# A table step at changes of ScalarE's function, and another order of the steps, in an attention and feed-forward kernel

## The chip, the cores and the metric

The kernel runs on one core of one Trainium2 chip. Its time is the device time of one execution in microseconds (us): the median of three runs, of which the lowest and the highest are given as well. A separate execution was taken by the hardware profiler; the rows below come from it. The engines are TensorE (PE for its matmuls, PEld for its weight loads), VectorE (DVE), ScalarE (ACT), GpSimd (POOL) and SyncE (SP, which issues nearly all transfers).

## What is computed

Two attentions after one another for 8 batches of 8 heads (576 rows of 64), then a feed-forward layer with a sigmoid gate over the 4608 rows of 512:

```python
p_packed = sm_attn(p, k, v)          # 32 packed queries look at 576 keys
out = sm_attn(q, p_packed, p_packed) # 576 queries look at the 32 packed rows
x = out.transpose(0, 2, 1, 3).reshape(B * S, H * D)
h = x @ w_in                         # 512 -> 2048
g = h * (1.0 / (1.0 + np.exp(-1.702 * h)))
return (g @ w_out)                   # 2048 -> 512
```

The softmax of `sm_attn` needs the function exp, the gate needs a gelu function. Both are done by ScalarE.

## The kernel before

All the work is one long list of steps, the tuple `order` (from line 931), written out by hand; a loop at the end calls them one by one. Each step puts a few instructions on one engine, and every engine works through its own instructions in that order. Nothing reorders them afterwards, so a step that waits holds up everything behind it on its engine.

A batch `b` goes through these steps. `load` brings k, q and v by DMA on SP's queue. `scores1_mm` (PE) makes the scores of the packed queries, `scores1_copy` moves them to SBUF, `scores1_max` and `bias1` (DVE) find the maxima, `exp1` (ACT) does the exponentials with the row sum. From batch 2 on `turn1_blocks` (DVE), `turn1_out` and `turn1_in` (eight small DMAs out to DRAM and two back) transpose them; then `pack` (PE) multiplies by v, `pack_end` scales, `pack_turn_mm` and `pack_turn_copy` transpose the result `PT`. `scores2_mm` (PE), `scores2_turn`, `max2`, `sub2` (DVE), `exp2` (ACT), `sum2`, `norm2`, `turn2` (DVE) are the second attention, up to its weights in `a` (`a_upper` by ACT, `a_lower` by DVE). `m_mm` (PE) multiplies `PT` by a quarter of w_in, which ACT and DVE then split in two parts (`m_upper`, `m_lower`).

The feed-forward layer runs in two phases of 1024 hidden columns each (first index of a step), per batch, half of the tokens (288) and one of four units `u` of 256 columns. `h_mm` (six matmuls for each half of a unit) fills one of two pairs of PSUM banks, which scores, `pack` and `m_mm` use as well. `g_main` and `g_over` (ACT) apply gelu to 256 and to the last 32 tokens; `g_sum`, `g_upper` (ACT) and `g_lower` (DVE) make and split the blocks of a Strassen-like product, and `prod` (PE) multiplies them by w_out into four accumulator banks A to D; `prod0` does the same plainly for batch 0. Tokens that `g_over` set aside are multiplied under the name "over". `c_take` keeps the sums of the first phase, `c_sum` and `c_comb` (DVE) add them in the second, `store` writes the output.

Weights come in as raw words: `load_w` (SP) into one of two buffers, `begin_w` (ACT) and `join_w` (DVE) turn them into fp32, which frees the buffer for the next `load_w`. `w_diff`, `wa_upper`, `wa_lower`, `wb_upper` and `wb_lower` split and combine w_out.

The function `table` (lines 121 to 123) applies a function to one column of a constant; it is called once, ahead of the list, with exp. Every other load of ScalarE's function table is put in by the compiler ahead of the first instruction that needs the other function.

Of the kernel before, what the change touches and what calls it, by code (L numbers as in the profile page):

```python
# [21 lines left out]
def kernel(  # L22
# [53 lines left out]
    cst = ctx.enter_context(tc.tile_pool(name="cst", bufs=1))  # L76
# [838 lines left out]
    def store(b, half, r=None, block=None, engine=nc.sync):  # L915
# [14 lines left out]
    table(AF.Exp)  # L930
# [34 lines left out]
        (exp2, 0, 1), (h_mm, 0, 0, 0, 0, 1, 1), (join_w, "in", 0, 0, 1), (wa_lower_mm, 0, 0),  # L965
        (load_w, "in", 1, 1, None), (g_main, 0, 0, 0, 0, 0), (sum2, 0, 1),
# [16 lines left out]
        (load_w, "out", 4, 0, None), (g_main, 0, 0, 1, 1), (g0_lower, 0, 0, 1),
        (prod0, 0, 1, 0, 1, 0), (begin_w, "in", 1, 3, None), (g_over, 0, 0, 1, 1),
        (prod0, 0, 1, 0, 0, 1), (g0_upper, 0, 1, 1), (join_w, "in", 1, 3, None),
        (load_w, "out", 5, 0, None), (prod0, 0, 1, 0, 1, 1), (g0_lower, 0, 1, 1), (m_mm, 0, 1),
        (t_store, 0, 1), (scores1_mm, 1, 0), (m_upper, 0, 1), (prod0, 0, 0, 1, 1),
# [795 lines left out]
```

## Time and profile before

| | |
|---|---|
| time, median of 3 runs | 668.72 us (668.45 to 670.74) |
| time of the profiled execution | 671.38 us |
| span of its instructions | 669.6 us |
| PE busy | 657.2 us (98%) |
| DVE busy | 552.0 us (82%) |
| ACT busy | 404.1 us (60%) |
| loads of the function table | 34, of 1.283 us each |

The span begins with the program's first instruction and ends with its last; 1.8 us of the profiled execution lie around it. The busy time of PE comes from modelled ends of pipelined matmuls. The granted clock of TensorE is 1.00 in all the stretches shown that end at 660 us or before, the upper of its two levels (2.4 GHz).

### The profile page before, as it was taken

The numbers are of one execution on the slowest core, as the hardware profiler recorded it, in microseconds if no ns is written. First come the engines' busy times: TensorE is split into PE (matmuls) and PEld (weight loads), VectorE is DVE, ScalarE is ACT, GpSimd is POOL, SyncE is SP. The second block draws the span as 40 slices with busy tenths as digits, with TensorE's granted clock in tenths as the row PEclk, the third lists the DMA queues.
The fourth block names the chain that finished last, engine by engine and source line by source line (L and its number), as shares of the span: only waits on it lengthen the run. The fifth ranks groups of instructions, "written<-read, shape, count | busy, mean of one in ns | idle before, by whom it ended". The sixth has DMA issues, their size and how long they took to land.

```text
span 669.6 us, 15216 instructions
## 1 busy us (share of the span) xinstructions
PE 657.2 (98%) x6227; PEld 597.8 (89%) x6227; DVE 552.0 (82%) x1132; ACT 404.1 (60%) x736; POOL 5.4 (1%) x15
## 2 busy tenths in 40 slices
PE   8999999999999999999999999999999999999997
PEld 6777798989989799798999789999999999999997
DVE  3958998788899887887887866888889978879897
ACT  5867877768576685875866664455444434444441
POOL 2100000000000000000000000000000000000000
PEclk9999999999999999999999999999999999999999
DMA  9876345563565828653576504232243242032422
GB/s 326 323 266 245 134 127 212 149 229 111 153 259 118 305 58 239 216 146 106 176 272 225 183 23 137 101 106 73 105 157 103 56 161 80 32 115 84 143 101 112
DMA packets 59173, 104.91 MB, mean 157 GB/s; under 512 B 31392, under 2 KB 36128, under 8 KB 58208
## 3 DMA queue, kind: packets, MB, share of 16 engines
q1 hardware_dynamic: 58960, 103.81, 47.3%
q8 instruction: 49, 0.80, 0.5%
q14 instruction: 20, 0.16, 0.1%
q10 hardware_dynamic: 144, 0.13, 0.1%
HBM read 70.51 MB, written 33.42 MB: 155 GB/s over the span
## 4 chain that ended last, share of the span: by engine, by line
PE 79%; DVE 8%; ACT 6%; DMA 5%; issue 2%; SPq 0%; ACTq 0%; DVEq 0%
PE h L699 25%; PE accC L860 11%; PE accB L860 11%; PE accA L860 11%; PE accD L860 6%; PE psm_None L547 4%; DMA raw_in_None<-w_in 2%; PE accB_over L860 1%; PE accC_over L860 1%; PE accA_over L860 1%; PE pspv_None L496 1%; PE ps L591 1%; DMA aT<-aside 1%; ACT L719 1%; PE accA L816 1%
## 5 line engine op out<-in xcount | busy, mean ns | idle before, releaser
L699 PE MATMUL h<-a,m 128*128 128x288 f32 x1536 | 226.3, 296 | 1.3 <-ACT over L725 0.6
L699 PEld LDWEIGHTS h<-a,m 128*128 128x128 f32 x1536 | 208.9, 188 | 7.2 <-ACT over L725 1.5
L111 ACT CAST gs<-X 128x896 fp32r<-128x896 f32 (+2 forms) x117 | 105.1, 903 | 70.9 <-DVE X L769 30.2
L789 DVE TENSOR_TENSOR gs<-X,gs 128x896 fp32r<-128x896 f32 x112 | 120.8, 1087 | 25.9 <-ACT gs L111 25.4
L769 DVE TENSOR_TENSOR X<-X 128x256 f32<-128x256 f32 (+1 forms) x336 | 105.2, 330 | 27.0 <-ACT X L719 23.1
L719 ACT ACTIVATE X<-h 128x512 f32<-128x512 f32 (+1 forms) x129 | 75.9, 595 | 71.6 <-PE h L699 45.7
L860 PE MATMUL accB<-Wb,gs 128*128 128x256 f32 x672 | 95.7, 281 | 0.0
L860 PE MATMUL accC<-Wa,gs 128*128 128x256 f32 x672 | 95.4, 281 | 0.0
L860 PEld LDWEIGHTS accC<-Wa,gs 128*128 128x128 f32 x672 | 86.0, 188 | 6.0 <-issue 4.7
L860 PEld LDWEIGHTS accB<-Wb,gs 128*128 128x128 f32 x672 | 86.6, 188 | 2.7 <-issue 1.8
L860 PE MATMUL accA<-Wa,gs 128*128 128x256 f32 x336 | 58.6, 282 | 0.2 <-DVE gs L789 0.2
L860 PE MATMUL accA<-Wb,gs 128*128 128x256 f32 x336 | 57.7, 280 | 0.0
L860 PE MATMUL accD<-Wa,gs 128*128 128x256 f32 x336 | 56.4, 282 | 0.1
L860 PEld LDWEIGHTS accD<-Wa,gs 128*128 128x128 f32 x336 | 46.8, 188 | 5.1 <-issue 4.3
L725 ACT ACTIVATE over<-h 128x64 f32<-128x64 f32 x128 | 34.9, 287 | 26.2 <-PE h L699 25.7
L860 PEld LDWEIGHTS accA<-Wa,gs 128*128 128x128 f32 x336 | 47.9, 188 | 2.8 <-issue 1.3
L860 PEld LDWEIGHTS accA<-Wb,gs 128*128 128x128 f32 x336 | 47.4, 188 | 0.0
L111 ACT CAST m<-psm_None 128x1024 fp32r<-128x1024 f32 x31 | 30.8, 1018 | 14.5 <-PE psm_None L547 14.3
L571 DVE TENSOR_TENSOR m<-psm_None,m 128x1024 fp32r<-128x1024 f32 x31 | 37.4, 1213 | 2.6 <-ACT m L111 2.4
L547 PE MATMUL psm_None<-w_in,PT 64*32 64x512 f32 x496 | 32.4, 596 | 1.3 <-DVE w_in L242 0.9
L665 DVE TENSOR_TENSOR a<-xt,a 128x576 fp32r<-128x576 f32 x31 | 23.1, 749 | 1.8 <-ACT a L111 1.7
L111 ACT CAST a<-xt 128x576 fp32r<-128x576 f32 (+1 forms) x30 | 19.8, 661 | 6.5 <-DVE xt L645 4.0
(203 smaller groups left out, 790.2 us busy)
## 6 DMA issues: line engine op xcount, KB each, us to landing
part<-r SPq DMA_DIRECT2D x14, 896.0 KB, 7.3
p<-part SPq DMA_DIRECT2D x14, 896.0 KB, 5.3
q<-q SPq DMA_DIRECT2D x16, 576.0 KB, 4.6
o<-r SPq DMA_DIRECT2D x16, 512.0 KB, 6.4
raw_out_None<-w_out SPq DMA_DIRECT2D x16, 511.8 KB, 4.7
v<-v SPq DMA_DIRECT2D x7, 1024.0 KB, 9.0
raw_in_None<-w_in SPq DMA_DIRECT2D x12, 511.8 KB, 4.7
k<-pk SPq DMA_DIRECT2D x8, 640.0 KB, 4.4
```

What stands on the lines that cost most here:

```text
L111: nc.scalar.copy(dst, src)
L496: nc.tensor.matmul(bank[32 * j : 32 * j + 32, e, e * D : (e + 1) * D], turned()[:, c, e, 32 * j : 32 * j + 32], vt[:, c, e0 : e0 + D], sta ...
L547: nc.tensor.matmul(banks[eo][32 * j : 32 * j + 32], PT[rows(eo), j, :], w_in_sb[c % 2][rows(eo), j, at], start=True, stop=True,)
L571: nc.vector.tensor_tensor(m[:, 1, :, at], st["bank", "m", b, c, part], m[:, 0, :, at].bitcast(F32), op=ALU.subtract,)
L591: nc.tensor.matmul(bank[32 * j : 32 * j + 32, eo, :NH], st["PT", b][rows(eo), j, :], kq["q0", half][rows(eo), j, :] if b == 0 else kq["q", ...
L665: engine.tensor_tensor(even_odd(a[:, 1], eo), even_odd(st["t", 2, b, half], eo), even_odd(a[:, 0], eo).bitcast(F32), op=ALU.subtract,)
L699: nc.tensor.matmul(h, m[:, part, eo, at], a[:, ap, eo * NH : (eo + 1) * NH], start=(n == 0), stop=(n == len(terms) - 1), skip_group_check= ...
L719: nc.scalar.activation(X[:, :4].rearrange("p (f t) n -> p f (t n)", f=2)[:, chunks(f)], st["h", *k][:, chunks(f), :NM], AF.Gelu_apprx_sigm ...
L725: nc.scalar.activation(over_part(ph, b, half, u), st["h", ph, b, half, u][:, :, NM:NH], AF.Gelu_apprx_sigmoid, scale=2.0,)
L769: engine.tensor_tensor(to, a, b_, op=ALU.subtract)
L789: engine.tensor_tensor(lo, X, hi.bitcast(F32), op=ALU.subtract)
L860: nc.tensor.matmul(acc[:, n * HC : (n + 1) * HC], gs[:, gp, g], Wa[:, wp, w] if w < 4 else Wb[:, wp, w - 4], start=(u == 0 and n == 0 and ...
```

## The change

`table` becomes a step of the list. It applies exp or gelu to one column of the constant `ident` and writes a column of its own, so that it waits for no other engine; nobody reads what it writes. 33 such steps are put into the list, 17 with "gelu" and 16 with "exp". The steps behind some 150 at the start stand in another order; the steps are otherwise the same, with the same arguments, so the matmuls, casts and transfers are the same in number and size. Followed along ScalarE's own steps, the new list has 34 changes of function, as many as the old one. Of these 34 loads one belongs to the call ahead of the list, 18 now fall on a table step and 15 still on the function itself; 15 of the 33 table steps ask for the function that is there already.

The core of the diff: the new function; the opening; batch 1's two attentions; batch 5's transposition; the end.

```diff
-    def table(func):
-        t = cst.tile([P, 1], F32, name="table")
-        nc.scalar.activation(t, ident[:, :1], func)
+    tables = {"exp": AF.Exp, "gelu": AF.Gelu_apprx_sigmoid}
+    primed = cst.tile([P, 2], F32, name="table")
+
+    def table(f):
+        n = list(tables).index(f)
+        nc.scalar.activation(primed[:, n : n + 1], ident[:, :1], tables[f])
...
-    table(AF.Exp)
+    table("exp")
...
-        (prod0, 0, 0, 0, 0, 1), (join_w, "in", 0, 3, 1), (a_upper, 0, 0, 1),
-        (join_w, "in", 1, 0, None), (load_w, "in", 1, 2, None), (prod0, 0, 0, 0, 1, 1),
-        (a_lower, 0, 0, 1), (begin_w, "in", 1, 1, None), (m_mm, 0, 0, 1),
-        (join_w, "in", 1, 1, None), (h_mm, 0, 0, 1, 0, 0), (load_w, "in", 1, 3, None),
-        (m_upper, 0, 0, 1), (wa_upper, 1, 0, 4, dve), (m_lower_mm, 0, 0, 1), (h_mm, 0, 0, 1, 0, 1),
-        (wa_lower, 1), (m_lower_copy, 0, 0, 1), (load, "v", 1, 3), (h_mm, 0, 0, 0, 1, 0),
...
-        (load_w, "out", 5, 0, None), (prod0, 0, 1, 0, 1, 1), (g0_lower, 0, 1, 1), (m_mm, 0, 1),
-        (t_store, 0, 1), (scores1_mm, 1, 0), (m_upper, 0, 1), (prod0, 0, 0, 1, 1),
...
+        (exp2, 0, 1), (table, "gelu"), (h_mm, 0, 0, 0, 0, 1, 1), (join_w, "in", 0, 0, 1),
...
+        (join_w, "in", 0, 3, 1), (prod0, 0, 0, 0, 1, 1), (a_upper, 0, 0, 1), (m_mm, 0, 0, 1),
+        (prod0, 0, 0, 0, 0, 1), (m_upper, 0, 0, 1), (m_lower_mm, 0, 0, 1), (m_lower_copy, 0, 0, 1),
+        (begin_w, "in", 1, 1, None), (join_w, "in", 1, 0, None), (a_lower, 0, 0, 1),
+        (h_mm, 0, 0, 1, 0, 0), (h_mm, 0, 0, 1, 0, 1), (wa_upper, 1, 0, 4, dve), (wa_lower, 1),
+        (join_w, "in", 1, 1, None), (g_over, 0, 0, 1, 0), (g_main, 0, 0, 1, 0),
...
+        (w_diff, 0, 2), (w_diff, 1, 1), (w_diff, 1, 3), (g0_lower, 0, 1, 0), (w_diff, 1, 2),
+        (load_w, "in", 1, 2, None), (load_w, "in", 1, 3, None), (load, "v", 1, 3),
...
+        (join_w, "in", 1, 3, None), (scores1_mm, 1, 0), (m_mm, 0, 1), (g0_upper, 0, 1, 1),
+        (scores1_copy, 1, 0, 0, dve), (scores1_copy, 1, 0, 1), (g0_lower, 0, 1, 1),
+        (wb_upper, 1, 0, dve), (scores1_mm, 1, 1), (m_upper, 0, 1), (scores1_copy, 1, 1, 1),
+        (scores1_copy, 1, 1, 0), (table, "exp"), (scores1_max, 1, 1), (bias1, 1, 1),
...
+        (prod0, 0, 0, 3, 1), (max2, 1, 1), (sub2, 1, 0), (table, "exp"), (wb_upper, 2, 0),
+        (prod0, 0, 1, 2, 0), (wb_lower, 2, 0), (wb_upper, 1, 1), (exp2, 1, 0), (g0_upper, 0, 1, 3),
+        (m_upper, 1, 1), (wb_upper, 0, 1), (m_upper, 1, 0), (wb_upper, 0, 0), (sum2, 1, 0),
+        (g0_lower, 0, 1, 3), (norm2, 1, 0), (prod0, 0, 1, 3, 0), (sub2, 1, 1), (turn2, 1, 0),
+        (m_lower, 1, 0), (c0_take, 0, 1), (a_upper, 0, 1, 0), (a_lower, 0, 1, 0), (c0_take, 0, 0),
+        (h_mm, 0, 1, 0, 0, 0), (h_mm, 0, 1, 0, 0, 1), (m_lower, 1, 1), (exp2, 1, 1),
+        (table, "gelu"), (g_main, 0, 1, 0, 0), (sum2, 1, 1), (g_sum, 0, 1, 0, 0, 1),
+        (g_sum, 0, 1, 0, 0, 2), (g_sum, 0, 1, 0, 0, 3), (h_mm, 0, 1, 0, 1, 0),
...
-        (g_upper, 0, "over", 0, 2, 0, 3), (g_sum, 0, 4, 0, 0, 2), (turn1_blocks, 5, 1),
...
-        (g_main, 0, 4, 0, 2), (turn1_blocks, 5, 0), (norm2, 4, 1), (turn2, 4, 1),
...
-        (pack, 5), (g_over, 0, 4, 1, 1), (g_sum, 0, 4, 0, 3, 3), (g_upper, 0, 4, 0, 3),
...
+        (c_take, 3, 1, "B"), (scores1_mm, 5, 0), (scores1_mm, 5, 1), (scores1_copy, 5, 0, 1, dve),
+        (scores1_copy, 5, 1, 1), (table, "exp"), (g_lower, 0, "over", 0, 2, 3, 7),
+        (scores1_max, 5, 1), (g_sum, 0, "over", 0, 3, 1), (bias1, 5, 1), (exp1, 5, 1),
+        (g_sum, 0, 4, 0, 0, 1), (g_sum, 0, "over", 0, 3, 2), (prod, 0, "over", 0, 1, "C"),
+        (prod, 0, "over", 0, 0, "B"), (prod, 0, "over", 0, 0, "A"), (turn1_blocks, 5, 1),
+        (prod, 0, "over", 0, 1, "D"), (prod, 0, "over", 0, 2, "C"), (prod, 0, "over", 0, 1, "B"),
+        (scores1_copy, 5, 1, 0), (scores1_copy, 5, 0, 0), (g_sum, 0, "over", 0, 3, 3),
+        (scores1_max, 5, 0), (g_sum, 0, 4, 0, 0, 2), (bias1, 5, 0),
+        (g_upper, 0, "over", 0, 3, 3, 7), (g_sum, 0, 4, 0, 1, 1), (norm2, 4, 1),
+        (g_sum, 0, 4, 0, 1, 2), (exp1, 5, 0), (g_upper, 0, "over", 0, 3, 0, 3, dve),
+        (turn1_blocks, 5, 0), (h_mm, 0, 4, 0, 3, 0), (h_mm, 0, 4, 0, 2, 0),
+        (prod, 0, "over", 0, 1, "A"), (table, "gelu"), (turn2, 4, 1),
...
+        (g_sum, 0, 4, 1, 0, 3), (turn1_in, 5, 0), (turn1_in, 5, 1), (pack, 5), (pack_end, 5),
+        (prod, 0, 4, 0, 1, "A"), (pack_turn_mm, 5), (pack_turn_copy, 5, dve),
...
-        (prod, 1, "over", 1, 3, "D"), (c_sum, "over", 1, "B"), (c_comb, "over", 1, 1),
-        (c_sum, "over", 1, "D"), (c_comb, "over", 1, 2), (prod, 1, "over", 1, 0, "C", 0),
-        (prod, 1, "over", 1, 0, "C", 1), (prod, 1, "over", 1, 1, "C", 0),
-        (prod, 1, "over", 1, 2, "C", 0), (c_comb, "over", 1, 3), (prod, 1, "over", 1, 3, "C", 0),
-        (c_comb, "over", 1, 4), (c_sum, "over", 1, "C", 0), (store, 7, 1), (store, "over", 1, 0),
-        (prod, 1, "over", 1, 1, "C", 1), (prod, 1, "over", 1, 2, "C", 1), (store, "over", 1, 1, 0),
-        (c_comb, "over", 1, 5), (prod, 1, "over", 1, 3, "C", 1), (c_sum, "over", 1, "C", 1),
-        (store, "over", 1, 1, 1, act),
...
+        (c_sum, 7, 1, "C"), (c_sum, "over", 1, "A"), (c_sum, "over", 1, "B"),
+        (prod, 1, "over", 1, 0, "D"), (prod, 1, "over", 1, 0, "C", 0), (store, 7, 1),
+        (prod, 1, "over", 1, 1, "C", 0), (prod, 1, "over", 1, 2, "C", 0),
+        (prod, 1, "over", 1, 3, "C", 0), (prod, 1, "over", 1, 1, "D"), (prod, 1, "over", 1, 2, "D"),
+        (prod, 1, "over", 1, 3, "D"), (c_comb, "over", 1, 0), (c_comb, "over", 1, 4),
+        (c_comb, "over", 1, 1), (c_sum, "over", 1, "C", 0), (store, "over", 1, 1, 0),
+        (c_comb, "over", 1, 2), (c_sum, "over", 1, "D"), (c_comb, "over", 1, 3),
+        (store, "over", 1, 0), (c_comb, "over", 1, 5), (prod, 1, "over", 1, 0, "C", 1),
+        (prod, 1, "over", 1, 1, "C", 1), (prod, 1, "over", 1, 2, "C", 1),
+        (prod, 1, "over", 1, 3, "C", 1), (c_sum, "over", 1, "C", 1), (store, "over", 1, 1, 1, act),
```

## Rows read from the trace of the kernel before

**Rows 1.** The page, busy time and share of the span by engine.

```profile
PE 657.2 (98%) x6227; PEld 597.8 (89%) x6227; DVE 552.0 (82%) x1132; ACT 404.1 (60%) x736; POOL 5.4 (1%) x15
```

**Rows 2.** Busy time by stretch (length, PE, PEld, DVE, ACT, POOL, clock, DMA share, GB/s).

```profile
40.00:120.00 80.00, 77.47 (x822) 62.86 (x811) 70.86 (x144) 62.07 (x114) 0.00 (x0) 1.00 0.55 183
...
200.00:300.00 100.00, 97.48 (x1032) 89.23 (x1031) 83.13 (x173) 71.91 (x126) 0.00 (x0) 1.00 0.61 181
300.00:660.00 360.00, 360.00 (x3071) 339.98 (x3070) 299.86 (x601) 185.51 (x329) 0.00 (x0) 1.00 0.36 120
660.00:669.60 9.60, 5.38 (x44) 4.97 (x42) 5.15 (x12) 0.00 (x0) 0.00 (x0) 0.91 0.30 110
```

**Rows 3.** PE in order of time: start, duration, work [idle before <-releaser].

```profile
41.38 0.62 PE L547 MATMUL psm_None<-w_in,PT 64*32 64x512 f32 x2 [0.91 <-DVE w_in L242]
...
53.05 1.87 PE L699 MATMUL h<-a,m 128*128 128x288 f32 x12 [0.40 <-ACT over L725]
...
73.22 1.89 PE L699 MATMUL h<-a,m 128*128 128x288 f32 x12 [0.48 <-DVE m L571]
...
85.94 0.38 PE L860 MATMUL accA<-Wa,gs 128*128 128x256 f32 x1 [0.23 <-DVE gs L789]
...
117.48 0.72 PE L292 MATMUL ps<-k 64*32 64x288 f32 x16 [0.35 <-ACT X L719]
...
219.19 1.32 PE L496 MATMUL pspv_None<-v,aT 128*32 128x64 f32 x80 [1.01 <-DMA aT<-aside]
```

**Rows 4.** PE in order of time, its last five microseconds of work.

```profile
660.72 1.58 PE L860 MATMUL accD_over<-Wa,gs_over 128*128 128x256 f32 x12
662.14 1.92 PE L860 MATMUL accC_over<-Wa,gs_over 128*128 128x256 f32 x15
664.59 1.32 PE L860 MATMUL accC_over<-Wa,gs_over 128*128 128x256 f32 x9 [0.53 <-DVE r_over L899]
```

**Rows 5.** Groups by line, table loads (count | busy us, mean ns | idle before, releasers).

```profile
L719 ACT ACT_TABLE_LOAD x10 | 12.8, 1283 | 5.2 <-PE h L699 5.1
...
L628 ACT ACT_TABLE_LOAD x9 | 11.5, 1283 | 2.9 <-DVE x L624 2.8
...
L389 ACT ACT_TABLE_LOAD x7 | 9.0, 1283 | 5.8 <-DVE nb L373 5.8
...
L725 ACT ACT_TABLE_LOAD x7 | 9.0, 1283 | 1.7 <-DVE gs_over L789 1.5
```

**Rows 6.** ACT in order of time, around two table loads.

```profile
81.77 1.28 ACT L389 ACT_TABLE_LOAD   x1 [0.82 <-DVE nb L373]
83.06 0.78 ACT L389 ACTIVATE x<-x,nb 128x576 f32<-128x576 f32 x1
...
114.30 1.28 ACT L719 ACT_TABLE_LOAD   x1 [2.71 <-PE h L699]
```

**Rows 7.** The chain of waits (start, duration, what) around a table load.

```profile
66.13 0.08 ACT L628
66.21 1.21 issue
```

**Rows 8.** DVE in order of time, ahead of the matmul at 73.22 us.

```profile
68.14 0.75 DVE L633 TENSOR_REDUCE sm<-x 128x18 f32<-128x576 f32 x1 [1.10 <-ACT x L628]
```

**Rows 9.** The chain of waits through w_in's buffers.

```profile
31.57 0.70 DVE w_in L242
...
32.29 7.46 DMA raw_in_None<-w_in
```

**Rows 10.** DVE in order of time, the two steps that split w_out for unit 1.

```profile
32.18 0.69 DVE L113 CAST Wa<-E 128x1024 fp32r<-128x1024 f32 x1
32.90 1.23 DVE L252 TENSOR_TENSOR Wa<-E,Wa 128x1024 fp32r<-128x1024 f32 x1
```

**Rows 11.** The page, DMA issues: size, median time to landing.

```profile
v<-v SPq DMA_DIRECT2D x7, 1024.0 KB, 9.0
```

**Rows 12.** Groups by line, the nearest one to a table step.

```profile
L358 ACT ACTIVATE again<-mx,nb 128x1 f32<-128x1 f32 x2 | 0.6, 284 | 0.0
```

More of the change, by code (lines that the diff above doesn't have):

```diff
@@ new lines @@
+        (begin_w, "out", 4, 0, None), (w_diff, 0, 4), (join_w, "out", 4, 0, None),
+        (h_mm, 0, 0, 0, 2, 0), (h_mm, 0, 0, 0, 2, 1), (exp1, 1, 0), (begin_w, "out", 5, 0, None),
+        (join_w, "out", 5, 0, None), (wb_lower, 1, 0), (h_mm, 0, 0, 1, 2, 0), (g_main, 0, 0, 0, 2),
+        (h_mm, 0, 0, 1, 2, 1), (prod0, 0, 1, 1, 0), (wa_upper, 2, 0, 4, dve), (load, "v", 1, 2),
+        (load, "q", 1, 0), (g0_upper, 0, 0, 2, None, dve), (wa_lower, 2), (g0_lower, 0, 0, 2),
+        (g_over, 0, 0, 0, 2), (g_over, 0, 0, 1, 2), (turn1_last_mm, 1), (g_main, 0, 0, 1, 2),
@@ new lines @@
+        (begin_w, "out", 7, 0, None), (join_w, "out", 7, 0, None), (h_mm, 0, 0, 1, 3, 0),
+        (pack_end, 1), (pack_turn_mm, 1), (wa_upper, 3), (g0_lower, 0, 0, 3), (pack_turn_copy, 1),
+        (w_diff, 2, 4), (h_mm, 0, 0, 1, 3, 1), (g_over, 0, 0, 1, 3), (g_main, 0, 0, 1, 3),
+        (table, "gelu"), (scores2_mm, 1, 0), (load, "q", 1, 1), (wa_lower, 3), (scores2_mm, 1, 1),
+        (prod0, 0, 0, 3, 0), (prod0, 0, 0, 2, 1), (scores2_turn, 1, 0, 1), (scores2_turn, 1, 0, 0),
+        (scores2_turn, 1, 1, 1), (scores2_turn, 1, 1, 0), (m_mm, 1, 1), (m_mm, 1, 0), (max2, 1, 0),
@@ new lines @@
+        (a_lower, 0, 2, 0), (load, "v", 3, 3), (m_lower, 2, 1), (exp2, 2, 1), (load, "k", 3, 0),
+        (h_mm, 0, 2, 0, 1, 0), (h_mm, 0, 2, 0, 1, 1), (load, "k", 3, 1), (t_store, 1, 0),
+        (table, "gelu"), (g_main, 0, 2, 0, 1), (g_over, 0, 2, 0, 1), (begin_w, "in", 2, 0, None),
+        (h_mm, 0, 2, 0, 0, 0), (h_mm, 0, 2, 0, 0, 1), (g_over, 0, 2, 0, 0), (table, "gelu"),
+        (g_main, 0, 2, 0, 0), (prod, 0, 1, 1, 2, "B"), (scores1_mm, 3, 1), (sum2, 2, 1),
+        (norm2, 2, 1), (g_sum, 0, 2, 0, 1, 1), (load, "v", 3, 2), (c_store, 1, 0),
@@ new lines @@
+        (exp2, 3, 1), (table, "exp"), (g_upper, 0, 2, 1, 3), (load, "k", 4, 0), (m_lower, 3, 0),
+        (t_store, 1, 1), (c_store, 1, 1), (load, "k", 4, 1), (a_lower, 0, 3, 0), (m_lower, 3, 1),
+        (h_mm, 0, 3, 0, 0, 0), (h_mm, 0, 3, 0, 0, 1), (table, "gelu"), (h_mm, 0, 3, 0, 1, 0),
+        (h_mm, 0, 3, 0, 1, 1), (g_main, 0, 3, 0, 0), (g_over, 0, 3, 0, 0), (g_lower, 0, 2, 1, 3),
+        (prod, 0, 2, 1, 3, "C"), (table, "gelu"), (g_main, 0, 3, 0, 1), (g_over, 0, 3, 0, 1),
+        (sum2, 3, 1), (g_sum, 0, 3, 0, 0, 1), (scores1_mm, 4, 1), (g_sum, 0, 3, 0, 0, 2),
@@ new lines @@
+        (wa_upper, 6), (m_upper, 0, 3), (m_lower, 0, 3), (m_upper, 1, 2), (m_lower, 1, 2),
+        (w_diff, 6, 1), (w_diff, 6, 3), (w_diff, 5, 4), (wa_lower, 6), (prod0, 1, 0, 1, 0),
+        (prod0, 1, 1, 1, 1), (h_mm, 1, 0, 0, 3, 0), (h_mm, 1, 0, 0, 3, 1), (h_mm, 1, 0, 0, 2, 0),
+        (g_over, 1, 0, 0, 3), (h_mm, 1, 0, 0, 2, 1), (g_main, 1, 0, 0, 3), (g0_upper, 1, 0, 3),
+        (g0_lower, 1, 0, 3), (wb_lower, 5, 0), (wb_upper, 4, 1), (g_main, 1, 0, 0, 2),
+        (g_over, 1, 0, 0, 2), (h_mm, 1, 0, 1, 2, 0), (h_mm, 1, 0, 1, 2, 1), (m_mm, 1, 3),
```

1446 lines of the change are left out of this document (697 added, 749 removed).

## The prediction

> **What bounds the kernel now.** I read first the busy shares: PE is busy 657.2 of 669.6 us, DVE 82%, ACT 60% [rows 1]. The reader sees that only PE's idle time can be won, since no matmul is removed. Second, the stretches: PE is idle 80 - 77.47 = 2.53 us between 40 and 120 us, 2.52 between 200 and 300, nothing between 300 and 660, and 4.22 behind 660 [rows 2]. The opening 40 us are left out, as their steps hardly move. Third, PE's own list, to see what ended each wait [rows 3]: it waits for weights at 41.38 (0.91 us), for ScalarE's gelu at 53.05 (0.40), for DVE's split of m at 73.22 (0.48), for a split block at 85.94 (0.23), for gelu at 117.48 (0.35), and for the transposed exponentials from DRAM at 219.19 (1.01). At the end it waits 0.53 us for `c_sum` [rows 4], and 3.69 us (4.22 less 0.53) of closing work follow its last matmul. So 2.53 + 2.52 + 0.53 = 5.58 us is all that shows as a wait behind 40 us.
>
> A wait costs somewhat more than the idle time shows, since matmul ends are modelled. In the last rows twelve matmuls take 662.14 - 660.72 = 1.42 us, 0.118 each; fifteen more would end their starts at 663.91, but the next start is at 664.59, 0.68 later where 0.53 is shown [rows 4].
>
> **The change, part by part. The loads of the table.** There are 34 before, all of 1.283 us [rows 5], and 34 after, by following exp and gelu along ScalarE's steps in both lists. So nothing is removed. What a table step can do is start a load while ScalarE waits for the data of the function. Before, some loads start only behind that wait: at 81.77 ScalarE has sat idle 0.82 us for `bias1`, loads, and begins exp at 83.06, 0.01 us after the load's end; at 114.30 it had idled 2.71 us for `h_mm` [rows 6]. All idle time ahead of the loads is 5.2 + 2.9 + 5.8 + 1.7 = 15.6 us, and a load can hide at most 1.283 of its own wait. That is ScalarE's time, which is no bound. What reaches PE must be read wait by wait:
>
> - 53.05: `g_over` comes late behind batch 1's two exp1 and two loads. After, exp is loaded behind the score copies; seven such loads before idled 5.8 us [rows 5], about 0.8 each, more than PE's 0.40. I take 0.40, though the gelu load that follows stays at its function.
> - 73.22: the chain runs through the load at 66.13 (0.08 + 1.21) [rows 7] and DVE's 1.10 us wait for exp2 [rows 8] to `m_lower`. After, the load stands ahead of exp2, with `wb_lower` in DVE's gap. I take 0.48.
> - 85.94: the load at 81.77 moves into its 0.82 us of wait [rows 6]. I take 0.23.
> - 117.48: the load at 114.30 had room for all its 1.283 [rows 6]. I take 0.35.
>
> Together -1.5 us. Ends: 0 (something else is late by as much) and -2.1 (0.15 more each). Late next at each is the same work without its load: PE's own queue, or DVE, whose busy share there is 70.86 of 80 [rows 2].
>
> The Trainium skill's page ScalarE: Activation LUTs (Table sets: the hidden batching unit) says that what counts is the number of switches, so calls should be batched by set. By that rule this part is worth 0, the sum without it stands below as a rival. The rows disagree in part: a load is 1.283 whenever it comes, but two of the ones shown come behind idle time.
>
> **Table steps that load nothing.** 15 of the 33 ask for the table that is there. The nearest row is an ACTIVATE on one column with a bias column, 0.284 us [rows 12]; 15 x 0.284 = 4.3 us of ScalarE. The cover is ScalarE's idle time, 17.9 of 80 us between 40 and 120 and 28.1 of 100 between 200 and 300 [rows 2]; without it each would delay by its 0.284 what PE waits for. I take 0; the ends are 0 and +4.3, a gain is excluded since they remove no load. The same page (What ACT_TABLE_LOAD costs) gives 186 ns for an ACTIVATE with immediate scale and bias; by that estimate it would be 15 x 0.187 = 2.8. No run here shows that form.
>
> **Batch 5's transposition.** `pack` waited 1.01 us for `turn1_in` [rows 3]. The new list moves exp's load ahead of the maximum, puts `turn1_blocks` well ahead (between the last of them and `pack`, PE has 14.9 us of matmuls by its pitches, against 7.8 before), and gives PE nine more products between the second `scores1_mm` and `pack`, 9 x 0.118 = 1.06 us. SP's queue has the same eight small DMAs and the q load ahead of `turn1_in`. I take -1.0; ends 0 and -1.2.
>
> **The end.** Before, DVE's `c_sum` of bank C's first half stands behind a queue of combinations when PE wants that bank. After, three D groups, 9 x 0.118 = 1.06 us, stand between the first half's last product and the second half, more than the 0.68 of wait. The closing work is the same. I take -0.6; ends 0 and -0.7.
>
> **The weights at 41.38.** This gets worse. The chain is `join_w` of w_in's tile 1 (31.57 to 32.27), which frees a buffer, then the DMA of tile 3, 7.46 us [rows 9], then its own begin, join and `m_mm`. After, that first `join_w` stands behind `wa_upper` (0.69) and `wa_lower` (1.23) of unit 1 on DVE [rows 10], and its `begin_w` behind the split of m on ACT. Queued behind it are SP's tile 3 and the v load; `m_mm` waits for that. The load leaves some 1.5 us later (1.92 less the half microsecond that DVE had idle). On PE `scores1_mm` now stands ahead of `m_mm` and covers 0.6. I take +0.9. Ends: 0, if the load lands sooner because k is then out of the way, and +3.1, if it takes the 9.0 us of a v load [rows 11] instead of 7.46 (1.5 + 1.5).
>
> **The rest of the order.** What is left, 5.58 - 0.40 - 0.48 - 0.23 - 0.35 - 1.01 - 0.53 - 0.91 = 1.67 us, are other waits. Counted over both lists with PE's pitches, a pair of banks is wanted again within 1.4 us of PE's work in 24 places before and in 21 after, so the new order is about as tight as the old one. I take 0; ends -1.7, all of them gone, and +2, as many new ones.
>
> **Sum.** -1.5 - 1.0 - 0.6 + 0.9 = -2.2 us. The profiled execution, 671.38 us (span 669.6 and 1.8 around it), would become 669.2. The median is 2.66 us below that execution, so the forecast is 668.72 - 2.2 = 666.5 us. On its own it reaches from 664.8 to 668.4.
>
> **The rivals.** *All waits go.* Every wait behind 40 us is filled by the new order: 668.72 - 5.58 = 663.1 us (down to 661.6 if all of them cost 0.68/0.53 of what shows). For it: PE without a wait from 300 to 660 us shows that an order can do this. Against it: the weight chain, and 15 loads that still stand at their function.
>
> *The tables give nothing.* The count of loads is what matters, or another thing is late at each place: 668.72 - 1.0 - 0.6 + 0.9 = 668.0 us. For it: DVE is nearly full between 40 and 120 us. Also in this case: the change doesn't do what it says, as 15 steps load nothing.
>
> *The early load gets in the way.* A table step loads at its place in ScalarE's queue, ahead of casts that PE or DVE need: the one of batch 1 stands in front of `wb_upper` and both `m_upper`. If four of the 18 hold up PE by their whole 1.283, it is +5.1 and the tables give nothing: 668.0 + 5.1 = 673.1 us, slower. It decides from the point where ScalarE has no idle time between the step and PE's next wait for it. For it: most loads before show no idle time ahead of them. Against it: ScalarE is idle 22% and 28% of the time in those stretches [rows 2].
>
> **How the numbers follow.** Forecast 0.46, all waits go 0.25, tables nothing 0.18, load in the way 0.11. The range of 8 in 10 leaves out the upper part of the slow case and the lowest of the fast one: 662.3 to 670.8. This kernel's measurement can tell about 0.5% from no change, 3.3 us: below 665.4 is faster, above 672.1 slower. Faster takes 0.24 of the fast case and 0.08 of the forecast's lower end, 0.32; slower nearly all of the slow case, 0.10; the rest, 0.58, is same.
>
> **What would show it.** Right: 34 loads still, those at a table step starting directly behind the instruction before; PE's idle time between 40 and 120 us near 2.0 and between 200 and 300 near 1.5; no wait at `pack` of batch 5 nor in the last matmuls; a wait near 1.8 at `m_mm` of w_in's second quarter. Wrong: new PE waits of over half a microsecond behind 300 us; casts on ScalarE that wait behind a table load while PE waits for them; a load of tile 3 that lands behind 43 us.

## The result and the profile after

The changed kernel takes 662.17 us (661.84 to 662.21, 4 runs) beside 669.08 (668.45 to 670.74, 4 runs) of the kernel before: a ratio of 0.9892 with a 95% interval of 0.9873 to 0.9911, so 1.1% faster. The forecast was 666.5 us with a range from 662.3 up: the sign was right, the size was not, and the range was missed at its lower end. The most likely case was "same"; "faster" came. The profiled execution took 661.84 us, 660.1 of them the span.

First the busy shares of after, the line that answers to [rows 1], and the busy time by stretch that answers to [rows 2] (length, PE, PEld, DVE, ACT, POOL, clock, DMA share, GB/s):

```profile
PE 652.5 (99%) x6227; PEld 596.8 (90%) x6227; DVE 552.5 (84%) x1132; ACT 408.2 (62%) x769; POOL 5.4 (1%) x15
...
40.00:120.00 80.00, 79.84 (x844) 67.18 (x833) 72.24 (x145) 66.13 (x128) 0.00 (x0) 1.00 0.57 185
...
200.00:300.00 100.00, 99.76 (x1149) 91.45 (x1148) 82.39 (x171) 72.70 (x135) 0.00 (x0) 1.00 0.61 193
```

PE does the same 6227 matmuls. Between 40 and 120 us it is idle 0.16 us where it was 2.53, between 200 and 300 us 0.24 where it was 2.52. Two waits of over 0.15 us are left behind 40 us, out of the seven of [rows 3 and 4] and four others. They are, in PE's order of time (start, duration, work, idle before and what ended it):

```profile
59.17 0.72 PE L594 MATMUL ps<-q,PT 64*32 64x288 f32 x16 [0.16 <-ACT X L722]
...
265.07 1.09 PE L550 MATMUL psm_None<-w_in,PT 64*32 64x512 f32 x16 [0.24 <-DVE x L604]
```

The table loads of after by line, which answer to [rows 5] (count | busy us, mean ns | idle before, releaser):

```profile
L126 ACT ACT_TABLE_LOAD x18 | 23.1, 1283 | 0.3
...
L722 ACT ACT_TABLE_LOAD x6 | 7.7, 1283 | 0.7 <-PE h L702 0.7
...
L126 ACT ACTIVATE table<-ident 128x1 f32<-128x1 f32 x34 | 6.9, 202 | 0.2
```

There are 34 loads, as before, each of 1.283 us. The 18 on a table step have 0.3 us of idle time ahead of them all together. The idle time ahead of all loads in the body of the kernel falls from the 15.6 us of [rows 5] to 2.8. A table step itself takes 0.202 us.

### The profile page after: what moved, and what is told of

It reads as the page before. It is cut to its first block, busy times and chain, and to the rows that moved or that the text cites. A ratio compares the mean times of both kernels' runs of the same rounds, so it can differ in the third digit from the quotient of the medians.

```text
span 660.1 us, 15282 instructions
## 1 busy us (share of the span) xinstructions
PE 652.5 (99%) x6227; PEld 596.8 (90%) x6227; DVE 552.5 (84%) x1132; ACT 408.2 (62%) x769; POOL 5.4 (1%) x15
## 4 chain that ended last, share of the span: by engine, by line
PE 96%; ACT 1%; DVE 1%; DMA 1%; issue 0%; SPq 0%
PE h L702 30%; PE accA L863 12%; PE accC L863 12%; PE accB L863 12%; PE accD L863 6%; PE psm_None L550 4%; PE accB L819 2%; PE accD L819 2%; PE accA_over L863 2%; PE accC_over L863 2%; PE accB_over L863 2%; PE accC L819 2%; PE accA L819 2%; PE ps L594 1%; PE pspv_None L499 1%; PE ps L295 1%
```

## The experiments

All times are medians, each beside runs of the kernel before on the same chip (669.7 to 670.1 us there). Two terms are used below: a load stands *at its function* when the compiler puts it there, and a step stands *directly ahead* when it is the last step before the function.

### The order or the steps?

The first question was which half of the change gives the gain. **The new order without its table steps**, `n1_after_no_table`:

```diff
+    order = [s for s in order if s[0] is not table]
```

> The changed kernel without its 33 table steps, its order otherwise kept; all loads of the function table fall back on the functions. Theory 'order': the waits went because every step has more work between it and what it waits for; without the table steps the time stays near 662 (661.5 to 663.5 us), PE's idle time behind 40 us stays under 1 us. Theory 'tables': the early loads carry the gain that the forecast had for them (1.5 us) or more; the time rises to 663.7 to 667 us, and PE waits again for gelu or exp near 50, 75, 85 and 117 us.

It took 668.30 us (668.11 to 670.01; ratio 0.9978, 0.9965 to 0.9992). The order alone is worth 1.5 us. PE waits in its trace on the work behind a load at its function, longer than before (the first is the matmul that waits 0.48 us at 73.22 in before) or anew, for instance:

```profile
70.60 1.64 PE L702 MATMUL h<-a,m 128*128 128x288 f32 x10 [0.89 <-ACT r L111]
...
85.46 0.74 PE L863 MATMUL accC<-Wa,gs 128*128 128x256 f32 x4 [0.83 <-DVE gs L792]
...
111.62 0.77 PE L702 MATMUL h<-a,m 128*128 128x288 f32 x4 [0.74 <-DVE m L574]
```

**The old order with a table step directly ahead of each of the 33 changes**, `n2_before_table_at_function`; `needs` names the function of each ScalarE step:

```diff
...
+    now, steps = "exp", []
+    for s in order:
+        f = needs.get(s[0], now)
...
+        if f != now:
+            steps.append((table, f))
+        now = f
+        steps.append(s)
+    order = steps
```

> The kernel before with one table step directly ahead of each of its 33 changes of function, nothing else moved: a load can then start while ScalarE waits for the function's data, and can hold up nothing but that function. Theory 'tables': the waits of rows 3 that were put down to loads (0.40, 0.48, 0.23, 0.35) go, 1.5 to 3 us faster than the kernel before, 666 to 667.5 us. Theory 'order': 0 to 1 us faster.

It took 664.71 us (663.97 to 667.30; ratio 0.9928, 0.9905 to 0.9950). **The same with the new order**, `n4_after_table_at_function`, drops the steps of after and puts one directly ahead of each change:

> The changed kernel with its 33 table steps taken out and one put directly ahead of each change of function: no idle table step is left, and every load can use its own wait. Theory 'order': the same as the changed kernel within 0.7 us, since PE waits only 0.4 us behind 40 us in it. Theory 'tables': places matter, up to 1.5 us either way.

It took 663.73 us (663.59 to 665.23; ratio 0.9909, 0.9890 to 0.9929). **The old order, with only its first part** (up to the scores of batch 2) **in the new order and without table steps**, `h1_first_part`; `place` is a step's index in the new order:

```diff
...
+    n = order.index((scores1_mm, 2, 0))
+    order = sorted(order[:n], key=place.get) + list(order[n:])
```

> The kernel before without any table step, but with all its steps up to the first scores of batch 2 (some 340 steps, up to about 78 us) in the relative order of the changed kernel; the rest as before. Theory 'order, all over': the four waits of that stretch (0.91, 0.40, 0.48 and about 0.2) go, 2 to 3 us faster than before. Forecast as written: the wait for w_in gets 0.9 longer and the others stay without table steps, so 0 to 1 us slower.

It took 671.24 us (670.19 to 674.21; ratio 1.0020, 1.0004 to 1.0036), slower than before. Its matmul at 70.74 waits 0.89 us, where before waits 0.48 for the same one at 73.22, and one at 79.64 waits 1.40 us that does not wait in before. So the steps are the larger half: 5.1 us in the old order, 6.1 in the new (668.30 to 662.17). The new order's early part is even a loss without them. Order and steps directly ahead are worth 1.5 and 5.1 us alone and 6.1 together (669.85 to 663.73), which the intervals do not tell from the sum; the places of after give some 1.6 us more (663.73 to 662.17).

### Which steps?

In the trace of before twelve of the 33 loads have over 0.1 us of idle time ahead of them, 15.3 us together. The other 21 start at most 0.02 us behind the instruction before. **Steps at the twelve only** (`n9_before_table_at_twelve`) and **at the 21 only** (`n10_before_table_at_the_rest`), both in the old order:

```diff
...
+    idle = (1, 3, 5, 8, 9, 16, 17, 18, 20, 23, 28, 29)
...
+        if f != now:
+            if n in idle:
+                steps.append((table, f))
+            n += 1
...
```

> The order of before, with a table step directly ahead of the function at only 12 of the 33 changes: those whose load in the trace of before has over 0.1 us of idle ahead of it (15.3 us in the twelve). With a step at all 33 this order took 664.71 against 669.85, 5.1 less. Theory (a load that the compiler places shares the wait of its function and so starts only when that wait ends; a step without waits starts it at once): the twelve carry the whole gain, 664.5 to 665.0, and the 21 other steps give nothing. Rival 1 (any step helps, because it shifts ScalarE's work or splits the change): a gain in proportion to the number of steps, 12/33 of 5.1, so 668.0. Rival 2 (only the four waits of the matmuls that stood behind a late load in the trace, 73.22, 85.94, 117.48 and 281.95, 1.6 us together): 668.2.

> The order of before, with a table step directly ahead of the function at the other 21 changes, whose load already started at most 0.02 us behind the instruction before it. Theory: there is nothing to win there, since the load cannot start earlier than it does; the 21 steps cost ScalarE 21 x 0.202 = 4.2 us of busy time, which lies in its idle 40%: 669.6 to 670.5 beside 669.85. Rival 1 (any step helps): 21/33 of 5.1, so 666.6. Rival 3 (a step delays the function behind it by its 0.2 us, and some matmul waits for that function): up to 2 us slower, 671.8.

The twelve took 664.42 us (663.92 to 666.13; ratio 0.9919, 0.9901 to 0.9938), which is all of the gain of 33. The 21 took 670.37 (668.87 to 674.40; ratio 1.0012, 0.9994 to 1.0029), no gain. Both rivals that reckon by the number of steps, or by the waits seen, are out. ScalarE's order of time around one of the twelve, the load that the chain of [rows 7] runs through, first in before:

```profile
62.75 0.60 ACT L111 COPY r<-accA 128x512 f32<-128x512 f32 x1
66.13 1.28 ACT L628 ACT_TABLE_LOAD   x1 [2.78 <-DVE x L624]
67.42 0.69 ACT L628 ACTIVATE x<-x 128x576 f32<-128x576 f32 x1
```

and with the step:

```profile
61.82 0.61 ACT L111 COPY r<-accA 128x512 f32<-128x512 f32 x1
62.44 1.28 ACT L126 ACT_TABLE_LOAD   x1
63.73 0.20 ACT L126 ACTIVATE table<-ident 128x1 f32<-128x1 f32 x1
65.23 0.69 ACT L631 ACTIVATE x<-x 128x576 f32<-128x576 f32 x1 [1.29 <-DVE x L627]
```

Here is the mechanism. This load, placed by the compiler, waits for what its function waits for: ScalarE sat idle 2.78 us for DVE's x, and only then came the 1.28 us. With a step that waits for nothing the load runs inside that wait, and the function still waits 1.29 us for DVE, so the whole load is off the path.

Not every load at its function does so. Five of the 21 others start directly behind the instruction before, and the function behind them does the waiting, over 0.1 us each. In before, of the same kind as the one above:

```profile
262.75 1.28 ACT L628 ACT_TABLE_LOAD   x1
266.35 0.69 ACT L628 ACTIVATE x<-x 128x576 f32<-128x576 f32 x1 [2.32 <-DVE x L624]
```

Such a load lies inside the wait already, and a step has nothing to give. What makes one load wait and another not is not shown by any run.

What that does to PE is seen by laying the two traces side by side, since PE's order is the same in both. First before, two waits beside those of [rows 3]:

```profile
281.95 1.20 PE L292 MATMUL ps<-k 64*32 64x288 f32 x32 [0.56 <-ACT over L725]
292.02 1.06 PE L699 MATMUL h<-a,m 128*128 128x288 f32 x6 [0.22 <-ACT over L725]
```

then the same matmuls, and some of [rows 3 and 4], with the twelve steps:

```profile
52.15 1.85 PE L702 MATMUL h<-a,m 128*128 128x288 f32 x12 [0.62 <-ACT over L728]
...
71.65 1.73 PE L702 MATMUL h<-a,m 128*128 128x288 f32 x12
...
277.21 1.20 PE L295 MATMUL ps<-k 64*32 64x288 f32 x32
...
286.88 0.96 PE L702 MATMUL h<-a,m 128*128 128x288 f32 x6
...
659.35 1.33 PE L863 MATMUL accC_over<-Wa,gs_over 128*128 128x256 f32 x9 [0.53 <-DVE r_over L902]
```

The lead over before is 53.05 - 52.15 = 0.90 us at the first, then 73.22 - 71.65 = 1.57, 4.74, 5.14 and, at the last matmuls, 664.59 - 659.35 = 5.24. The 0.90 is the wait at 41.38 us of [rows 3], which has nothing to do with the tables (below). The rest, 4.3 us, comes behind the loads that stood idle, in a dozen small parts, and a wait that goes gives more than PE's idle time showed: the lead grows by 0.67 where 0.48 was shown at 73.22.

**The 15 steps that load nothing**, taken out of after (`n6_after_no_idle_table`), and **a step directly ahead at the 15 changes of after that have none** (`n15_after_step_at_all`). Both compare each table step, and each function, with the function loaded last; of the first:

```diff
...
+        f = s[1] if s[0] is table else needs.get(s[0], now)
+        if s[0] is not table or f != now:
+            steps.append(s)
...
```

> After without its 15 table steps that change nothing (the function's table is loaded already). Prediction's term: the 15 steps cost nothing: 662.0 to 662.4 beside 662.17. Rival 1 (each costs ScalarE its 0.202 us where something waits): 15 x 0.2 = 3.0 us at most, 659.2 to 661.5. Rival 2 (the places are part of the searched order; without them the scheduler's order of instructions on ScalarE shifts and waits appear): 662.5 to 663.5.

> After with a table step directly ahead of the function at each of its 15 changes that have none. Its loads still stand idle for 2.8 us together without the first (1.7 ahead of the row maximum's exp, 0.7 ahead of one gelu). Theory: a load that starts up to 0.7 us earlier in those two or three places gives at most half a microsecond: 661.6 to 662.2. Rival (those loads are covered by other work, the 15 steps cost nothing either): 662.0 to 662.3.

They took 662.04 us (661.94 to 663.16; ratio 0.9883, 0.9862 to 0.9903) and 662.10 (661.93 to 662.92; ratio 0.9881, 0.9860 to 0.9903): neither is to be told from after's 662.17. The idle steps cost nothing that shows, and an earlier start of the loads that are left gives nothing.

### What do the loads cost at all?

With exp in the place of gelu there is one load in the whole kernel. The output of the feed-forward part is then another function's. **After and before with one function**, of the two lines of ScalarE the first; in after the table steps ask for exp only as well:

```diff
...
-            st["h", *k][:, chunks(f), :NM], AF.Gelu_apprx_sigmoid, scale=2.0,
+            st["h", *k][:, chunks(f), :NM], AF.Exp, scale=2.0,
...
```

> After with exp in the place of gelu in both of its ScalarE lines, so that the function table is loaded once; the 33 table steps stand, without a load. The output of the perceptron is therefore another function's. ScalarE loses 33 x 1.283 = 42.3 us. Theory (in after the loads that remain lie in ScalarE's idle time): 660.5 to 662.2 beside 662.17. Rival (number counts: 30 more loads cost 32.9 us, 1.1 us each, so 33 fewer give a part of that back): below 658.

> Before with exp in the place of gelu in both of its ScalarE lines: one load in the whole kernel, and nothing else changed; the output of the perceptron is another function's. It gives the whole price of the 33 loads in the order of before. Theory (the price was their late start, and the twelve steps took nearly all of it): 663 to 664.5, little under the 664.42 of the twelve steps. Rival (the loads themselves cost PE time beyond their late start): 660 or less.

After took 661.43 us without its loads (661.13 to 661.61; ratio 0.9868, 0.9848 to 0.9889), before 663.19 (663.00 to 664.65; ratio 0.9894, 0.9870 to 0.9918). So the 33 loads cost 6.5 us in before, 669.72 to 663.19, and 0.7 in after. The twelve steps took 5.3 of the 6.5 away. Of the 0.7, the traces of after with and without loads show where: without them PE is 0.32 us ahead at 19.2 us, before the first of the 33, 0.66 at 28.7, behind it, and 0.73 at the end, so the other 32 cost next to nothing. The busy shares of after without loads:

```profile
PE 652.1 (99%) x6227; PEld 597.0 (91%) x6227; DVE 552.0 (84%) x1132; ACT 366.4 (56%) x736; POOL 5.4 (1%) x15
```

ScalarE has 408.2 - 366.4 = 41.8 us less to do, and PE is as busy as with the loads. The other end is **30 more loads**: each idle step of after preceded by a step for the other function, `n7_after_loads_in_pairs`:

```diff
...
+        if s[0] is table and f == now:
+            steps.append((table, "gelu" if f == "exp" else "exp"))
...
```

> After with each of its 15 idle table steps preceded by one of the other function: 30 more loads of 1.28 us and 15 more steps, 30 x 1.283 + 15 x 0.202 = 41.5 us more of ScalarE's time, and nothing else changed. It asks what ScalarE's time itself is worth, and so whether the number of loads or their place decides. Theory (place: a load costs PE only where somebody waits for what stands behind it; ScalarE is idle for 38% of the span): 3 to 15 us of the 41.5 reach the end, 665 to 677. Rival 1 (number: each load stops ScalarE and what waits for it, by its full length): 695 to 703.7. Rival 2 (ScalarE's idle time hides them whole): 662 to 663.

It took 695.09 us (694.85 to 698.90; ratio 1.0379, 1.0353 to 1.0404), 32.9 more than after, and my theory for it fell: its rival's figure came. 79% of the 41.5 us reached the end, though ScalarE is idle 38% of the span. ScalarE in order of time ahead of one of the new waits of PE, and that wait:

```profile
163.29 1.28 ACT L126 ACT_TABLE_LOAD   x1
164.58 0.20 ACT L126 ACTIVATE table<-ident 128x1 f32<-128x1 f32 x1
164.79 1.28 ACT L126 ACT_TABLE_LOAD   x1
166.08 0.20 ACT L126 ACTIVATE table<-ident 128x1 f32<-128x1 f32 x1
166.19 0.58 ACT L722 ACTIVATE X<-h 128x512 f32<-128x512 f32 x1
166.67 0.27 ACT L728 ACTIVATE over<-h 128x64 f32<-128x64 f32 x1
```

```profile
167.00 1.22 PE L295 MATMUL ps<-k 64*32 64x288 f32 x16 [2.95 <-ACT over L728]
```

PE wants back the pair of banks that gelu empties, and gelu stands behind two loads and two steps, 166.19 - 163.29 = 2.90 us; PE waits 2.95. A part of the 32.9 us is the clock's, which the expectation did not have. In this trace PE is idle 22.9 us behind 40 us (0.5 in after), and the granted clock is at its lower level, 1.2 GHz, in three stretches of 3.4 to 6.8 us, each beside a wait of 2.2 to 3.0 us. The stretch that holds the second half of one of them (clock third from the end, 1.00 being 2.4 GHz):

```profile
168.00:172.00 4.00, 4.00 (x31) 3.86 (x24) 3.72 (x11) 2.15 (x4) 0.00 (x0) 0.75 0.51 152
```

Set beside the same matmuls of after, an estimated 4.9 us are lost in the three where PE shows no wait. So a load costs 0.02 us (0.7 / 33) in the mean at the places of after, and 1.1 us (32.9 / 30, some 0.16 of it the clock) where ScalarE has work due. A mean idle share says nothing of which it is.

### Where ahead of the function?

**Each step as early as it can stand**, right behind the last use of the other function, in the old order (`n5_before_table_early`):

```diff
...
+        if f and f != now:
+            steps.insert(at, (table, f))
+        steps.append(s)
+        if f:
+            now, at = f, len(steps)
...
```

> The order of before, with a table step at all 33 changes, each as early as it can stand: right behind the last step that uses the other function. In this order the step directly ahead of the function gave 664.4 to 664.7; in the order of after, places ahead of the function gave 1.5 more than directly ahead (663.73 to 662.17). Theory: a load behind other waits of ScalarE starts still earlier here, and the two waits left behind loads (h behind over, 0.35 to 0.62 us at 52; ps behind X) shrink: 662.8 to 664.0. Rival 1 (a step directly ahead does all that a place can do in this order, the 1.5 belongs to the order of after): 664.4 to 664.8. Rival 2 (the prediction's third rival, the early load gets in the way: a load of 1.28 us ahead of casts and copies that PE waits for delays them, 33 times): slower than directly ahead, 665.5 to 668.

It took 674.91 us (674.47 to 677.56; ratio 1.0073, 1.0052 to 1.0094): slower than before, and 10.2 us slower than the same 33 steps directly ahead (664.71). ScalarE's order of time at one load, and PE's wait there:

```profile
75.13 0.60 ACT L722 ACTIVATE X<-h 128x512 f32<-128x512 f32 x1
75.75 1.28 ACT L126 ACT_TABLE_LOAD   x1
77.04 0.20 ACT L126 ACTIVATE table<-ident 128x1 f32<-128x1 f32 x1
77.15 0.68 ACT L111 COPY x<-ps 128x288 f32<-128x288 f32 x2
```

```profile
77.89 2.38 PE L702 MATMUL h<-a,m 128*128 128x288 f32 x16 [1.38 <-ACT x L111]
```

The load stands ahead of the copies that free the scores' banks. Directly ahead of the function, behind those copies, it falls into the wait for `bias1` instead, the 0.82 us of [rows 6]. This is what the prediction's third rival describes, in another kernel.

**One early place in the new order**: as `n4_after_table_at_function`, but the load ahead of batch 2's `exp2` keeps its place in after, six steps earlier (`n12_one_early_place`):

```diff
...
+        if s[0] is table:
+            if s[1] == "exp" and order[i + 6][:3] == (exp2, 2, 0):
+                steps.append(s)
+                now = "exp"
+            continue
...
```

> The order of after with table steps directly ahead of the function (663.73 by itself), but for one: the load ahead of batch 2's row softmax keeps the place that it has in after, six steps earlier, where ScalarE stands idle for 1.85 us behind its copies of r. In the trace of after that softmax's exp starts 1.6 us earlier (100.59 against 102.20), and the wait for m of 0.83 us at 108 is not there. Theory: this one place gives most of the 1.56 us between the two: 662.4 to 662.9. Rival 1 (the gain is spread over the 17 places): 663.5 to 663.7. Rival 2 (the wait moves on to another operand): 663.7, with a wait of about 0.8 us for another tile behind 108.

It took 662.42 us (662.18 to 664.32; ratio 0.9890, 0.9866 to 0.9914), so this one place gives 1.3 of the 1.6 us between directly ahead and after by the medians. The two intervals overlap (the ratio was 0.9890 to 0.9929 directly ahead), so the place rests on the traces as well. ScalarE with the load directly ahead, and the wait of PE behind it:

```profile
99.57 0.95 ACT L111 CAST gs<-X 128x896 fp32r<-128x896 f32 x1 [1.85 <-PE accD L863]
...
100.80 1.28 ACT L126 ACT_TABLE_LOAD   x1
...
102.20 0.67 ACT L631 ACTIVATE x<-x 128x576 f32<-128x576 f32 x1
```

```profile
108.05 2.24 PE L702 MATMUL h<-a,m 128*128 128x288 f32 x14 [0.83 <-DVE m L574]
```

and with the load in its early place:

```profile
99.62 1.28 ACT L126 ACT_TABLE_LOAD   x1
...
101.45 0.95 ACT L111 CAST gs<-X 128x896 fp32r<-128x896 f32 x1 [0.34 <-ACT table L126]
102.30 0.36 ACT L111 COPY r<-accD 128x256 f32<-128x256 f32 x1
102.64 0.69 ACT L631 ACTIVATE x<-x 128x576 f32<-128x576 f32 x1
```

The second execution runs 1.9 us behind the first here, mostly since the clock fell in its opening (last section); its exp starts 0.44 us later by the trace's time, and so some 1.4 us earlier beside the other work. The load moves out of the stretch between the copy of r and exp, where it was on the path to m, into the 1.85 us that ScalarE waits for the last accumulator ahead of them. The wait at 108 us is gone. The place wanted is thus a gap of ScalarE, not the earliest place nor always the last.

### Parts of the order

**Batch 5's transposition**, moved alone in the old order (`n8_before_blocks5`):

```diff
+    steps = [s for s in order if s != (turn1_blocks, 5, 0)]
+    steps.insert(steps.index((turn1_blocks, 5, 1)) + 1, (turn1_blocks, 5, 0))
...
```

> The order of before, with one step moved: the transposition of batch 5's first half (turn1_blocks of 5, 0) directly behind the second half's, where the transposed copy through the DRAM leaves earlier. In the traces of before and of its order with all table steps the first matmul of pack 5 waits for that DMA, 1.01 and 1.78 us; in the order of after it does not wait. Theory: this wait is a part of what the new order gives and a cause of the scatter of before (668.47 to 672.83): 668.6 to 669.0, with single times that lie closer together, and no wait over 0.3 us near 219 us. Rival (the wait goes, and the next thing on that path, the function or the table load there, takes its place): 669.5 to 670, the wait named behind another.

It took 669.89 us (669.09 to 670.87; ratio 0.9995, 0.9981 to 1.0009). No wait for the DMA is left at `pack`, though that alone proves little: in the profiled kernels that keep before's steps there, this wait was anywhere from 0 to 1.78 us. Eleven microseconds earlier there is a new one:

```profile
206.72 0.39 PE L860 MATMUL accA_over<-Wa,gs_over 128*128 128x256 f32 x1 [1.07 <-DVE gs_over L789]
```

The rival came: DVE does the transposition ahead of the block gs_over, which PE then misses by as much.

**The end** in the new order, beside the twelve steps (`n11_twelve_and_tail`):

```diff
...
+    n = order.index((prod, 1, "over", 1, 0, "A"))
+    order = list(order[:n]) + sorted(order[n:], key=place.get)
...
```

> The order of before with a table step directly ahead of the function at the twelve changes whose load stood idle (664.42 by itself), and the last stretch, from the products of batch 0's over on, in the order of after. In the traces of before and of its order with table steps the last matmuls wait 0.53 us for r_over near 660 to 664; in those of after's order there is no such wait. Theory: the wait goes and no other takes its place: 663.7 to 664.0, and the weight loads' idle time behind 600 us falls from 2.26 to about 1.5. Rival (another operand of the last matmuls is late next, or the closing work behind the last matmul takes longer): 664.3 to 664.6 with the closing over 3.7 us or a wait for another tile.

It took 663.86 us (662.58 to 664.89; ratio 0.9901, 0.9880 to 0.9921). Its last matmuls run without a wait where those of the twelve alone wait 0.53 us:

```profile
657.83 1.59 PE L863 MATMUL accC_over<-Wa,gs_over 128*128 128x256 f32 x12
```

The medians differ by 0.56 us, as expected, though their intervals overlap.

**The weights**: only the load of v's last part moved behind w_out's last load, in the old order (`n3_before_late_v_last`):

```diff
+    steps = [s for s in order if s != (load, "v", 1, 2)]
+    steps.insert(steps.index((load_w, "out", 5, 0, None)) + 1, (load, "v", 1, 2))
...
```

> The order of before with one transfer moved: the load of v's last part (256 KB), issued at 33.1 us behind the load of w_in's tile 3, goes behind the last load of w_out, where the order of after has it. Theory (it shares the DMA engines with tile 3's load and lengthens it): the load of tile 3 lands in 3.7 to 4.7 us (after: 3.71; before 7.46, and 5.4 to 6.5 in four kernels with before's issues), no wait near 41 us in the trace, and if that wait is what moves the median of before, 668.7 to 669.2 with fewer times above 671. Rival (the 1024 KB of v, which stay, are what it shares with, or the landing just scatters): 5.4 to 7.5 us, 669.5 to 670.2.

It took 670.93 us (668.82 to 673.27; ratio 1.0004, 0.9988 to 1.0019). The times to landing of the two loads of w_in issued between 30 and 34.2 us (minimum, median, maximum; the longest is tile 3's), first here, then in the kernel of the moved transposition, where no issue of this stretch was changed:

```profile
DMA to landing us min/median/max: 5.2/5.9/6.7
```

```profile
DMA to landing us min/median/max: 4.3/5.3/6.3
```

The theory fell: 6.7 us for tile 3 without v's last part behind it, 6.3 with it.

## Why the prediction was wrong

**The table loads: the step that failed.** The forecast took 1.5 us from four waits, with 2.1 as the end. The steps give 5.3 us in the old order (the twelve) and 6.1 in the new one. Three things were wrong with the term.

- It read the loss from PE's waits, wait by wait. A wait that goes gives more than its idle time: 0.67 us of lead for the 0.48 at 73.22. The forecast had that number in hand for the end (0.68 for 0.53) and allowed 0.15 a site.
- It took four sites of twelve. The lead of the twelve over before grows by 3.17 us between 73.22 and 281.95, which holds the sites at 85.94 and 117.48, forecast at 0.23 and 0.35, and seven more loads; the waits at 281.95 and 292.02 were in no term of their own.
- It costed the steps in the old order's waits only. Without steps the new order has longer ones, 0.89 us at 70.60 and 0.83 at 85.46, and the steps take those away as well.

ScalarE's own column would have held the size. The idle time ahead of the twelve loads, counted at 1.283 us at most for each, is 11.9 us in the trace of before; 5.3 of it reached PE. The forecast named the whole, 15.6 us, and set it aside because ScalarE is no bound; as the end of the term it would have put 662 within the range. The 53.05 that was taken at 0.40 is the opposite case: of the two loads ahead of it one had 0.42 us of idle time and the other none, and with the twelve steps PE still waits there, 0.62 us; with no loads at all (`n14_before_one_function`) that wait is gone.

The Trainium skill's page ScalarE: Activation LUTs (section Table sets: the hidden batching unit) lets the number of switches decide, and the forecast's second rival was built on it, at 668.0 us. The runs disagree on that: the same 34 loads stand in kernels of 669.7 and 664.4 us, by their start alone. Where loads fall into ScalarE's busy time the runs agree with it: 30 more of them took 32.9 us.

**The idle steps: right.** 0 taken; without them 662.04 beside 662.17, no difference in the noise. The nearest row was badly chosen: the trace of before has the very form once, in the call ahead of the list, at 0.188 us, against the 0.284 of [rows 12], and the forecast said that no run showed it. The end of +4.3 was therefore too wide, by that row 15 x 0.188 = 2.8.

**Batch 5's transposition: its wait went, its price is not shown apart.** In after no wait for the DMA is left at `pack`. The 1.01 us taken for it is one execution's, of a wait that the old order shows from 0 to 1.78. Moved alone, the step gives nothing, since gs_over is late instead. In the kernel with the new order and no table step that wait is gone as well; how much of that order's 1.5 us it is stays open.

**The end: its wait went, and the size fits.** -0.6 taken; 0.56 between the medians with and without it, less than their noise, and no wait in after.

**The weights: failed, in sign.** The load of tile 3 leaves 1.6 us later, as worked out (33.89 us where it was 32.29). It lands in 3.7 us and not in the 7.46 taken over from [rows 9], so the wait of 1.8 that the forecast wanted to see is not there. The rows of after for the same two loads:

```profile
DMA to landing us min/median/max: 3.7/4.2/4.6
```

The step that failed is the use of one execution's transfer time as a constant. Eight kernels with before's steps there showed 5.3 to 7.5 us for that load, and only the 7.5 of the profiled before had a wait of over 0.2 us behind it at 41 us. Eight with after's steps showed 3.6 to 3.9. What parts the two groups in the traces is the transfer of k ahead of it. In all of the first, k landed 1.1 to 1.8 us after the load had left (33.67 and 32.29 us in before); in all of the second, 0.1 to 1.6 us earlier (33.65 and 33.89 in after). The time of leaving alone does not decide it: in `n11_twelve_and_tail` the load left at 34.07, later than in after, but ahead of k's landing, and took 5.3 us. The forecast had this case as its end of 0, that k is out of the way, and took the other; its upper end, +3.1, comes to 3.0 by its own two terms. No run moves k alone, so it is what goes with the shorter transfer and not yet its shown cause; the transfer of v's last part was tried alone and is not it.

**The order as a whole: too small.** The whole order, without steps, gives 1.5 us (0.2%, interval 0.08 to 0.35%); the forecast's terms for it were -1.0 - 0.6 + 0.9 = -0.7.

**The rivals.** "All waits go" (663.1, down to 661.6) is what came, in kind as well: behind 40 us PE's shown waits are 0.16 and 0.24 us. It had a chance of 0.25. What spoke against it was the weight chain, where one scattered row was trusted, and the 15 loads still at their function, of which most have no idle time ahead to lose. "The early load gets in the way" did not come in after, but it is no ghost: at the earliest places it gave 674.91, near its 673.1.

**The account.** Old order 669.7; twelve steps 664.4; the end 663.9; the whole order, with a step directly ahead of all 33 changes, 663.7; one load six steps earlier 662.4; all places 662.2. The traces show 4.3 us for the twelve steps where the medians show 5.3. The old order without the twelve steps scatters by 1.8 to 5.5 us from run to run, after, in four runs, by 0.4, so the last microsecond may be what transfers cost in some runs; that was not settled.

## What to carry to other kernels

Of the loads of the function table that the compiler places, some begin only when an operand of their function is there, here twelve of 33; the trace tells which, by the idle time ahead of the load. There a one-column call of the function without waits, 0.2 us long, moves the load into that wait; where the load had none, the call gave nothing. Put it into a gap of the engine and not merely early: a load cost 0.02 us in the mean at the places of after, and 1.1 us ahead of work that PE waited for.

## What the runs showed of the hardware

- A table load that waits for nothing starts at most 0.02 us behind the instruction before it, and what follows and waits for nothing starts 0.01 us behind the load's end: above, the load at 62.44 follows the copy that ends at 62.43, and the step begins at 63.73. All loads of all kernels took 1.283 us.
- In the opening the clock falls in some executions and not in others; four of the profiled ones show it. The busy time by stretch of after without its idle steps, and of after:

```profile
12.00:14.00 2.00, 2.00 (x36) 1.64 (x27) 0.00 (x0) 0.61 (x3) 0.00 (x0) 0.50 1.07 401
```

```profile
12.00:14.00 2.00, 1.69 (x22) 0.90 (x22) 0.15 (x1) 1.42 (x6) 0.00 (x0) 1.00 1.08 404
```

The granted clock (the third number from the end) is at its lower level, 1.2 GHz, from 12 to 14 us in the one and at the upper in the other; the spans are 661.3 and 660.1 us. Ahead of it PE's waits for the first transfer and for ScalarE were longer in the first kernel:

```profile
6.64 0.72 PE L331 MATMUL ps<-k 64*32 64x288 f32 x16 [0.75 <-DMA k<-pk]
...
9.31 0.44 PE L424 MATMUL accB_pst<-ident,x 128*128 128x128 f32 x2 [0.68 <-ACT x L385]
```

In after the two were 0.43 and 0.45 us. The waits alone do not tell it: in the kernel with steps at the 21 they were 0.59 and 0.63 us, and the clock stayed at its upper level.
